# A sparse-attention and MLP kernel on one core: the whole list of steps in another order

## The chip, the cores and the metric

The kernel runs on one core of one Trainium2 chip. The metric is the device time of one execution, in microseconds (us). Five engines work beside each other, each through its own queue of instructions in order: PE (matrix products), DVE (vector work), ACT (activation functions and copies), POOL (vector work, and the issue of some DMAs), SP (the issue of the other DMAs). Sixteen DMA engines carry the transfers of both issuing queues.

## The reference: what is computed

Four batches of 8 heads, 768 positions, head size 64. Attention is local (a window of 16 positions to each side) plus 24 block keys per head (the maximum over a block of 32 keys) with block values (the mean over 32 values). Its output is 3072 tokens of width 512, which go through a two-layer MLP with a gelu in between:

```python
k_sum = k.reshape(B, H, nb, block, D).max(axis=3)
v_sum = v.reshape(B, H, nb, block, D).mean(axis=3)
scores_l = scale * q @ k^T,  kept where |i - j| < 16
scores_s = scale * q @ k_sum^T + log(32)
a = softmax(concat(scores_l, scores_s))
x = (a @ concat(v, v_sum)).transpose(0, 2, 1, 3).reshape(3072, 512)
h = x @ w_in                              # 512 -> 2048
out = (h / (1 + exp(-1.702 * h))) @ w_out # 2048 -> 512
```

## The kernel before, in words

The work goes batch by batch: turn keys and queries so that the head size lies on the partitions, scores, exponentials, values, x turned, then `x @ w_in`, gelu, and `@ w_out`. The attention of one batch is placed beside the MLP of the batch ahead of it, so that PE always has matmuls to do.

**The order is a list.** A string `ORDER` (lines 35 to 111) holds 1002 steps. The last lines of the kernel split it at blanks and call, for each word, a small function from the table `ops` with the numbers of the word as arguments. The class `_Ordered` (lines 18 to 30) wraps each engine and keeps every instruction in program order, so within an engine the list is the order of execution. Between engines only data and buffers decide. Every recorded row carries line 28, the line of the wrapper; the rows are told apart by tile names.

**The steps that the change and the prediction touch.** The first number after a name is mostly the batch.

- Loads, all issued by POOL on one software queue: `Lk`, `Lq`, `Lv` (keys, queries, values of batch 0; `load_k0`, `load_q0`, `load_v0`), `Li.0` to `Li.4` and `Lo.0` to `Lo.3` (parts of w_in and w_out), `lk.b.h`, `lq.b.h` (one head of keys or queries, 96 KB each on chip), `lv.b.j.e` (a part of the values, 64 KB). Key and query tiles of two halves are used again batch after batch. In the trace an issue on this queue waits until the one eight places ahead of it has landed.
- `gate.1`: a small POOL copy that reads the last sum row of batch 1, so that POOL issues no load behind it before that row has landed. `gate.2` does the same with the last turned x.
- `tk`, `tq` (`turn_k`, `turn_q`): keys and queries of batch 1 turned on PE; `kc`, `qc` copy them out. `xm`, `kh`, `kr`: block maxima, halos and block rows of the keys of batch 1. For batches 2 and 3 SP turns them by DMA: `xk.s.g.e` (keys, tile `kx`), `xq.s.g` (queries, tile `qT`), both for the heads of group g. There `xa.g` takes the block maxima on DVE, `ka` copies the halos, `kR` (`rows_all`) writes the maxima in.
- `s.b.half.p` (`scores`), `e` (exponentials on ACT), `m` (mask on DVE), `v.b.half.p` (values on PE, tile `ps_av`), `nn` (normed on DVE), `t`/`c` (x turned on PE and copied) or `d` (x turned by a DMA on SP).
- `vm.b` (`vsum`, 48 short matmuls) and `vb` (`block_sums`, five DVE instructions) make the block values `vs`. SP then copies them into the value tile: `sd.b.e` (sum rows) and `ha.b.i` (halo copies within the value tile `vw`). For batch 1 the list has the four halos ahead of the two sum rows. The values of a batch need all six copies.
- `f.half.nt` (`ff`): a column block of `x @ w_in`, four matmuls; `g`: its gelu on ACT.
- The product with w_out is done by seven half-size products instead of eight: `p.t.what` (`product`, 8 matmuls; tiles `poA`, `poB`, `poC`), `x.t.what` (`taken`), with sums of gelu outputs `gs.j.n.what` (`g_sums`, DVE or POOL) and of weights `ws.what.part` (`w_sum`, DVE). Product 1 and 2 need no sum; 6, 5, 7 and 3 read the sums 1, 0, 2 and 3 of all blocks, the last of which is `gs.7.1.*`. Product 2 reads the last two parts of w_out (`Lo.2`, `Lo.3`), and `ws` reads all four.
- `o`: a store on SP. `G`, `X`: the activation tables on ACT.

Of the kernel before, what the change touches and what calls it, by code (L numbers as in the profile page):

```python
# [35 lines left out]
start Lk.0 X Lk.1 id Lq.0.0 Lk.2 Lk.3 Lq.0.1 Lv.0 Lv.1 Lv.2 cs I.20.256 sel on T.0.2 Li.1 Lv.3 To.0.a ba I.2.128 km.0  # L36
sm.0.42 Li.0 sm.1.52 T.1.1 To.1.a Lq.1.0 Lq.1.1 I.3.128 Q.0.0.0 I.14.128 Qc.0.0.a Qc.0.1.d so.0 sx.0 km.1 T.2.1 To.2.a so.1
sx.1 T.3.0 em.2 ed.0 ex.0.1 ex.0.0 bt.0.1 bx.0 To.3.d Q.0.1.0 Qc.0.2.d sm.2.42 so.2 sx.2 Qc.0.3.d sm.3.52 Li.4 so.3
sx.3 km.2 vt.0.2.1 vc.0.2.d km.3 ao.0.40 ao.1.41 ab.0 ab.1 ae.1 ae.0 vn.0 vn.1 ed.1 ex.1.0 bt.1.0 ex.1.1 lh.3.g bx.1
vt.2.1.1 vc.2.1.d ao.2.2 xt.0.3 lh.0.d ab.2 xc.0.d lh.1.g ae.2 vn.2 vt.3.1.1 vc.3.1.a ao.3.1 ck.0 xt.1.3 lo.0.g lh.2.g  # L40
# [5 lines left out]
lk.1.2 lv.1.5.1 lk.1.5 lk.1.6 lq.1.2 lk.1.7 m.1.1 lq.1.1 lv.1.0.0 lq.1.4 lq.1.5 lq.1.7 lv.1.3.1 lq.1.6 lv.1.0.1
lv.1.2.0 lv.1.1.0 cv.1 lv.1.1.1 lv.1.4.0 lv.1.2.1 f.0.8.k0123.2 lv.1.4.1 late m.1.3 ws.0.0 g.0.8 f.0.9.k0123.3
f.0.11.k0123.0 g.0.9 f.0.10.k0123.1 v.0.1.0.40 v.0.1.1.41 lv.1.3.0 nn.1.0 g.0.11 lv.1.5.0 g.0.10 v.0.1.2.50 v.0.1.3.51
nn.1.1 f.0.12.k0123.2 g.0.12 f.0.13.k0123.3 g.0.13 t.1.0.42 c.1.0.d f.0.14.k0123.1 g.0.14 f.0.15.k0123.0 t.1.1.52
c.1.1.d f.1.0.k01.2 f.1.8.k01.3 f.1.1.k0123.1 ws.1.0 g.0.15 g.1.1 f.1.0.k23 ws.2.0 f.1.8.k23 g.1.0 g.1.8 ws.0.1 ws.1.1  # L50
# [30 lines left out]
x.1.3.a o.1.1.0.0.2 nn.0.1 d.0.1 p.2.1.2 x.2.1.d p.1.4 v.2.1.0.40 v.2.1.1.41 nn.1.0 x.1.4.d v.2.1.2.50 v.2.1.3.51
nn.1.1 p.2.5.1 x.2.5.a d.1.0 p.2.6 d.1.1 gate.2 lq.3.6 p.2.2.3 x.2.6.a p.2.7 x.2.7.a p.2.3 G x.2.2.a x.2.3.a
o.1.2.0.0.2 p.2.4 x.2.4.a f.0.1.k01.0 f.0.9.k01.3 f.0.0.k01.2 f.0.0.k23 xk.1.1.0 xk.1.0.1 f.0.8.k01.1 f.0.8.k23
f.0.1.k23 lv.3.5.1 lq.3.1 lq.3.2 g.0.0 g.0.8 g.0.1 o.1.1.1.0.2 f.0.9.k23 g.0.9 xk.1.1.1 xk.1.0.0 o.1.2.1.0.2 xq.1.1
f.1.0.k0123.2 g.1.0 f.1.8.k0123.1 g.1.8 f.1.1.k0123.0 xq.1.0 g.1.1 gs.0.2.2 f.1.9.k0123.3 g.1.9 f.0.2.k0123.2 g.0.2
# [879 lines left out]
```

## Time and profile before

| | |
|---|---|
| runs | 212.68, 215.77, 213.2 us; median 213.2 |
| span of the profiled execution | 212.3 us (0.4 below the lowest run) |
| PE busy | 199.1 us, 94% of the span |
| DVE, ACT, POOL busy | 127.8, 117.7, 108.6 us |
| DMA | 27.74 MB, 131 GB/s in the mean |

The page of the profile lists the busy time of each engine, then the span in 40 slices with the granted clock of PE (`PEclk`, in tenths of full speed), the DMA queues, the chain of waits (the work that ended last, followed back from the last instruction to what released it), and the costliest groups of instructions: mean duration, then the idle time of the engine ahead of them and what ended most of it. "issue" in the chain is time in which the engine waited for nothing that the profile shows. A timeline row gives the start, the length, the engine, the operation and the tiles; in brackets stands how long the engine sat idle before it and what released it. DMA rows give the time from the issue to the landing.

### The profile page before, as it was taken

How to read it: one execution, taken by the hardware profiler on the slowest of the kernel's cores; microseconds unless marked ns; L12 is line 12 of the kernel's file. 1: busy time of each engine (PE TensorE's matmuls, PEld its weight loads, DVE VectorE, ACT ScalarE, POOL GpSimd, SP SyncE). 2: the span in 40 equal slices, each digit the busy share in tenths (PEclk: the TensorE clock that was granted, in tenths of full speed). 3: DMA queues.
4: the chain of work that ended last, by engine and by line, in shares of the span. 5: the costliest groups of instructions: out<-in, count | busy, mean ns of one | idle time of the engine just before them, and what ended most of it. 6: DMA issues, size and time to landing. Idle time of an engine off the chain costs nothing.

```text
span 212.3 us, 5885 instructions
## 1 busy us (share of the span) xinstructions
PE 199.1 (94%) x2440; PEld 145.3 (68%) x2440; DVE 127.8 (60%) x311; ACT 117.7 (55%) x227; POOL 108.6 (51%) x157
## 2 busy tenths in 40 slices
PE   7888798989998899999699999999999999999992
PEld 5546555657886786656578876566888856668882
DVE  5557865799886861168976823496587602454242
ACT  2662886667865338766664048668660467670200
POOL 7999962399970989808949314331000009432000
PEclk9999999999999999999999999999999999999999
DMA  5999999999999799999999999992023930000222
GB/s 69 156 166 190 209 218 216 178 135 123 98 138 203 111 160 179 120 164 170 145 153 201 134 220 128 253 171 59 3 99 60 181 112 0 0 3 0 99 102 99
DMA packets 96458, 27.74 MB, mean 131 GB/s; under 512 B 85024, under 2 KB 93488, under 8 KB 96432
## 3 DMA queue, kind: packets, MB, share of 16 engines
q0 software_dynamic: 70800, 13.64, 85.7%
q1 hardware_dynamic: 25632, 13.74, 31.9%
q8 instruction: 19, 0.31, 0.7%
q14 instruction: 7, 0.06, 0.1%
...
## 4 chain that ended last, share of the span: by engine, by line
PE 72%; DMA 18%; POOL 4%; issue 2%; DVE 1%; SPq 0%; POOLq 0%
PE ph L28 31%; PE poA L28 19%; PE poB L28 9%; DMA w_out_sb<-in_moe_w_out_dram 7%; PE poC L28 5%; DMA kb<-in_k_dram 4%; DMA v0n<-in_v_dram 4%; DMA vw<-vs 3%; PE ps_av L28 3%; PE ps_s L28 2%; PE ps_t L28 1%; POOL kb L28 1%; PE ps_vs L28 1%; DVE vs L28 1%; POOL mk L28 1%
## 5 line engine op out<-in xcount | busy, mean ns | idle before, releaser
L28 PE MATMUL ph<-xT,w_in_sb 128*128 128x384 f16 x512 | 85.9, 326 | 0.0
L28 ACT ACTIVATE gT<-ph 128x384 f16<-128x384 f32 x128 | 58.7, 495 | 22.9 <-PE ph L28 21.9
L28 PEld LDWEIGHTS <-w_in_sb 128*128 128x128 f16 x512 | 49.2, 98 | 31.5 <-DMA w_in_sb<-in_moe_w_in_dram 0.2
L28 PEld LDWEIGHTS <-gs 128*128 128x128 f16 x384 | 36.3, 98 | 4.7
L28 DVE TENSOR_TENSOR gs<-gT 128x768 f16<-128x768 f16 (+1 forms) x36 | 17.1, 490 | 21.5 <-ACT gT L28 21.4
L28 PEld LDWEIGHTS <-gT 128*128 128x128 f16 x288 | 27.5, 98 | 3.7
L28 ACT ACTIVATE a_sb<-ps_s 128x768 bf16<-128x768 f32 x32 | 24.5, 808 | 9.1 <-PE ps_s L28 9.0
...
L28 POOL DMA_DIRECT2D kb<-in_k_dram x28 | 23.0, 836 | 8.1 <-DMA w_out_sb<-in_moe_w_out_dram 6.2
...
L28 PE MATMUL poA<-ws,gs 128*128 128x256 f16 x192 | 24.9, 273 | 0.0
L28 POOL TENSOR_TENSOR gs<-gT 128x768 f16<-128x768 f16 x4 | 6.9, 1728 | 35.0 <-ACT gT L28 35.0
L28 ACT ACTIVATE s<-poA 128x256 f32<-128x256 f32 x14 | 5.4, 384 | 20.6 <-PE poA L28 19.0
L28 DVE TENSOR_TENSOR x<-ps_av,rc 128x768 f16<-128x768 f32 (+1 forms) x18 | 15.6, 869 | 0.6
L28 DVE TENSOR_TENSOR a_sb<-a_sb,mk 128x768 bf16<-128x768 bf16 x28 | 14.6, 549 | 1.8 <-ACT a_sb L28 1.1
L28 POOL TENSOR_TENSOR gs<-gs,gT 128x768 f16<-128x768 f16 (+1 forms) x6 | 8.4, 1406 | 12.9 <-DVE gs L28 12.9
L28 DVE TENSOR_TENSOR gs<-gT,gs 128x768 f16<-128x768 f16 (+1 forms) x19 | 9.2, 490 | 7.2 <-POOL gs L28 6.6
L28 PE MATMUL poB<-ws,gs 128*128 128x256 f16 x96 | 12.5, 273 | 0.0
L28 PE MATMUL poB<-w_out_sb,gs 128*128 128x256 f16 x96 | 12.5, 273 | 0.0
L28 PE MATMUL poA<-ws,gT 128*128 128x256 f16 x96 | 12.5, 273 | 0.0
L28 PE MATMUL poC<-w_out_sb,gT 128*128 128x256 f16 x96 | 12.5, 273 | 0.0
L28 PE MATMUL poA<-w_out_sb,gT 128*128 128x256 f16 x96 | 12.3, 273 | 0.0
(102 smaller groups left out, 215.9 us busy)
## 6 DMA issues: line engine op xcount, KB each, us to landing
...
kb<-in_k_dram POOLq DMA_DIRECT2D x24, 96.0 KB, 5.7
qb<-in_q_dram POOLq DMA_DIRECT2D x24, 96.0 KB, 5.4
...
```

Of the source, the lines that this page charges most:

```text
L28: r = f(*a, **kw)
```

## The change

Only the string `ORDER` changes; it holds the same 1002 steps in another order. No function, tile, size or engine of a step is changed.

- Batch 0: all four `Lv` and both `Lq.1` are ahead of any `Li` (before: `Li.1` between `Lv.2` and `Lv.3`, `Li.0` ahead of `Lq.1`). `Lq.0.0` is behind `Lk.2`. The parts of w_in go 1, 0, 2, 3, 4 (before 1, 0, 4, 2, 3).
- w_out: `Lo.0`, `Lo.2`, `Lo.1`, `Lo.3` stand spread among the head loads of batch 1, the last of them behind sixteen (before: all four ahead of `lk.1.0`).
- Batch 1: `tk.0` and `tk.1` stand among the first steps of the second half of ff (before: in its middle); the weight sums `ws` go down to just ahead of their products. SP's copies go `ha.1.3`, `ha.1.0`, `ha.1.1`, `sd.1.1`, `ha.1.2`, `sd.1.0` (before: 3, 2, 1, 0, then the sum rows).
- Batch 2: its loads behind `gate.1` are mixed differently; `lk.2.5` is the 18th (before, the last key load was the 13th), and four parts of the values come last. First loads of batch 3 (`lv.3`) follow directly. `xk` goes 0.1.0, 0.1.1, 0.0.1, 0.0.0; two stores stand ahead of `xq.0.0`, a store and a halo ahead of `xq.0.1`. `vm.2` is six ff steps sooner. On DVE `vb`, one `gs`, `xa.0.0`, `xa.1.0`, `kR.0` stand together with most `gs` behind them; the first two scores are ahead of `p.0.1.2`.
- Batch 3: both `xa` and `kR.1` sooner, `vm.3` ten ff steps later, halos behind the sum rows or among them. In the tail the products are mixed differently; the last two steps are the same.

The diff around the keys of batches 1 and 2, cut to its core:

```diff
-sd.0.0.3 ha.0.2.3 sd.0.1.3 ha.0.3.3 ha.0.0.3 lk.1.0 f.0.0.k23 ha.0.1.3 Qc.1.3.d s.0.1.2.52 f.0.1.k01.3 e.1.2
-f.0.3.k0123.0 g.0.2 g.0.0 g.0.1 g.0.4 g.0.6 g.0.3 lk.1.3 lq.1.0 g.0.7 g.0.5 lq.1.3 ck.1 m.1.0 m.1.2 ow.1 lk.1.4 lk.1.1
-tk.0.52 kc.0.a f.1.13.k0123.0 g.1.13 ws.3.1 g.1.4 f.1.5.k0123.1 g.1.5 tk.1.52 gs.4.2.2 kc.1.a f.1.14.k0123.3 tk.2.42
-e.1.0 ha.1.1.0 x.1.1.d x.0.3.a lq.2.0 lq.2.2 lv.2.0.0 lq.2.3 kh.2.1.g p.0.4 ha.1.0.0 lv.2.5.0 o.0.0.0.0.2 x.0.4.a
-s.1.1.1.52 e.1.1 m.0.1 vm.1.42 vb sd.1.1.0 kr.2.1.g kh.3.1.d sd.1.0.0 xm.3.1 kr.3.1.d p.1.5.1 gate.1 lv.2.3.0 lv.2.1.1
-lk.2.0 m.1.1 m.0.0 lk.2.2 o.0.0.1.0.2 lv.2.2.0 lv.2.2.1 lk.2.3 lv.2.5.1 lk.2.1 x.1.5.d lk.2.4 lk.2.5 lk.2.7 lk.2.6
-g.0.0 g.0.8 g.0.1 g.0.9 xk.0.0.0 xk.0.0.1 xk.0.1.0 xk.0.1.1 xq.0.0 xq.0.1 f.1.0.k0123.2 f.1.8.k0123.1 g.1.0
-g.1.7 f.0.15.k0123.0 ha.2.3.0 g.0.15 gs.6.1.1 f.0.7.k0123.1 g.0.7 kR.0.d f.1.15.k0123.3 g.1.15 gs.7.1.0 X gs.6.1.3
-p.0.1.2 s.2.0.1.52 e.0.1 s.2.0.0.42 lv.3.1.0 lk.3.0 lk.3.4 lv.3.1.1 lk.3.2 gs.7.1.1 lk.3.7 lk.3.3 ha.2.1.0 x.0.1.d
...
+Li.3 lo.1.g mk.0 sx.3 vc.3.1.a ow.0 lk.1.0 ab.2 ae.2 vn.2 mk.1 cvs Li.4 xt.1.3 mf Qc.1.0.a ao.3.1 lv.1.1.1 cv.0 ab.3
+lk.1.1 Qc.1.3.d e.1.0 Lo.0 lq.1.0 lk.1.4 ha.0.1.3 lv.1.3.1 vo.1.d Qc.1.2.a lk.1.7 sd.0.0.3 f.0.1.k01.3 xt.3.1 s.0.1.1.42
+s.0.1.2.52 lk.1.6 xc.3.a f.0.0.k23 lq.1.1 lq.1.3 e.1.1 f.0.3.k0123.0 s.0.1.3.42 lk.1.5 f.0.2.k0123.1 Lo.2 lq.1.2 Lo.1
+g.0.14 f.0.15.k0123.0 g.0.12 t.1.1.52 t.1.0.42 f.0.13.k0123.3 c.1.1.d tk.0.52 g.0.13 c.1.0.d kc.0.a f.1.1.k0123.1
+sd.1.1.0 kr.3.1.d kh.3.1.d p.1.5.1 gate.1 p.2.1.2 ha.1.2.0 s.1.0.2.52 x.1.6.a e.0.2 s.1.0.3.42 x.1.5.d sd.1.0.0 p.1.3
+lk.2.7 f.1.9.k0123.3 g.1.0 f.1.1.k0123.0 g.1.9 lk.2.5 f.1.8.k0123.1 xk.0.1.0 f.0.2.k0123.2 g.1.8 f.1.11.k0123.3 g.0.2
+f.1.2.k0123.1 f.0.3.k0123.2 xk.0.1.1 g.1.1 g.1.11 lq.2.6 lv.2.3.1 xk.0.0.1 lv.2.2.1 f.0.10.k0123.0 g.1.2 f.1.10.k0123.3
+lv.2.5.1 g.0.3 g.0.10 lv.2.0.1 f.1.4.k0123.1 g.1.10 f.0.4.k0123.2 lv.3.2.0 f.1.12.k0123.3 f.0.11.k0123.0 g.1.4 xk.0.0.0
+o.0.1.1.0.2 gs.0.2.0 g.0.4 g.0.11 o.0.2.0.0.2 f.1.3.k0123.1 g.1.3 gs.2.2.0 vm.2.42 g.1.12 f.0.12.k0123.0 f.1.5.k0123.1
+f.0.6.k0123.2 gs.0.2.1.g g.1.13 g.0.13 g.0.6 g.1.6 vb gs.2.2.1 o.0.2.1.0.2 f.0.14.k0123.0 f.1.14.k0123.3 xa.0.0 ka.0.g
+f.1.7.k0123.2 xa.1.0 g.1.14 kR.0.d gs.4.2.2.d g.1.7 f.0.7.k0123.1 f.1.15.k0123.3 gs.4.2.0 g.0.14 gs.2.2.3 f.0.15.k0123.0
+lv.3.3.0 gs.6.1.0 ha.2.0.0 gs.6.1.1 g.0.7 g.1.15 xq.0.1 s.2.0.0.42 s.2.0.1.52 p.0.1.2 gs.7.1.0 g.0.15 gs.4.2.1 p.0.2.0
```

More of the change, by code (lines that the diff above doesn't have):

```diff
@@ L35 @@
 ORDER = """
[L36 to L40, printed above, removed]
@@ L46 @@
[L46 to L50, printed above, removed]
@@ L81 @@
[L81 to L85, printed above, removed]
@@ L106 @@
[L106 to L110 removed]
+start Lk.0 Lk.1 I.20.256 I.2.128 cs ck.1 Lk.2 id sel ba T.0.2 Lq.0.0 sm.0.42 I.3.128 To.0.a T.1.1 To.1.a Lk.3 Lq.0.1 X
@@ new lines @@
+f.0.8.k0123.2 g.0.1 lv.1.2.0 lv.1.1.0 lv.1.4.0 g.0.4 late f.0.10.k0123.1 m.1.3 f.0.11.k0123.0 g.0.10 v.0.1.0.40 lv.1.3.0
+v.0.1.2.50 v.0.1.1.41 nn.1.0 lv.1.5.0 v.0.1.3.51 nn.1.1 g.0.8 f.0.9.k0123.3 g.0.11 g.0.9 f.0.12.k0123.2 f.0.14.k0123.1
+g.0.14 f.0.15.k0123.0 g.0.12 t.1.1.52 t.1.0.42 f.0.13.k0123.3 c.1.1.d tk.0.52 g.0.13 c.1.0.d kc.0.a f.1.1.k0123.1
+f.1.0.k01.2 f.1.0.k23 f.1.8.k01.3 f.1.8.k23 g.1.1 tk.1.52 f.1.10.k0123.1 xm.0.1 g.0.15 g.1.8 g.1.0 kh.0.1.d kr.0.1.d
+ws.0.0 kc.1.a ha.1.3.0 kh.1.1.d f.1.9.k0123.0 g.1.9 lv.2.0.0 f.1.3.k0123.2 f.1.2.k0123.3 f.1.13.k0123.0 g.1.10 xm.1.1
@@ new lines @@
+gs.0.2.0 g.1.2 f.1.11.k0123.1 g.1.3 gs.0.2.2 g.1.13 f.1.12.k0123.3 f.1.4.k0123.2 tk.3.52 g.1.11 g.1.4 gs.0.2.1 tk.2.42
+f.1.5.k0123.1 gs.2.2.0 g.1.12 g.1.5 gs.2.2.2 gs.2.2.1 f.1.6.k0123.2 kc.3.d gs.0.2.3 f.1.14.k0123.3 ws.1.0 f.1.15.k0123.0
+gs.4.2.0 ws.2.0 g.1.6 gs.4.2.1 f.1.7.k0123.1 kc.2.a g.1.15 tq.0.42 g.1.14 g.1.7 p.0.1.2 tq.1.52 gs.6.1.2 ha.1.0.0
+gs.4.2.3 x.0.1.a qc.0.a gs.4.2.2 gs.7.1.0 ws.0.1 gs.6.1.0 ws.1.1 gs.6.1.1 lq.2.0 p.1.1.3 X p.0.2.0 gs.7.1.1 p.0.6
+tq.2.42 p.0.5.1 x.0.6.a gs.2.2.3 lq.2.2 gs.7.1.2 ws.2.1 p.0.7 gs.6.1.3 qc.1.a lq.2.3 ws.3.0 qc.2.a kr.1.1.d x.0.5.a
@@ new lines @@
+s.2.1.3.52 sd.2.0.0 m.1.1 e.1.3 lk.3.2 p.1.5.0 m.0.0 sd.2.1.0 x.1.1.a p.1.2.2 e.1.2 m.0.3 v.2.0.2.50 v.2.0.0.40
+v.2.0.3.51 x.1.5.d m.1.2 m.1.3 v.2.0.1.41 m.1.0 o.1.0.1.0.2 p.1.6 x.1.6.a nn.0.1 lk.3.3 x.1.2.a nn.0.0 p.1.3 p.1.7
+o.1.0.0.0.2 p.2.1.2 v.2.1.2.50 x.1.7.a G x.1.3.a v.2.1.3.51 v.2.1.0.40 v.2.1.1.41 x.2.1.d p.1.4 x.2.5.a d.0.0 p.2.6
+x.2.6.a nn.1.1 p.2.3 lv.3.1.0 lq.3.3 p.2.7 x.1.4.d lq.3.4 nn.1.0 p.2.2.3 o.1.1.0.0.2 lk.3.7 x.2.7.a d.0.1 p.2.4
+f.0.1.k01.0 x.2.2.a d.1.1 x.2.4.a f.0.9.k01.3 f.0.0.k01.2 f.0.0.k23 d.1.0 x.2.3.a g.0.0 f.0.1.k23 f.0.8.k01.1 f.0.9.k23
@@ new lines @@
+f.0.8.k23 f.1.0.k0123.2 g.0.1 lv.3.1.1 lq.3.7 g.0.8 g.1.0 f.1.1.k0123.0 lv.3.5.0 g.0.9 f.1.8.k0123.1 g.1.1 f.1.9.k0123.3
+g.1.8 f.0.10.k0123.0 f.1.2.k0123.1 xk.1.0.1 xk.1.0.0 g.0.10 f.0.2.k0123.2 lk.3.6 lv.3.0.1 o.1.2.0.0.2 xa.0.1 o.1.2.1.0.2
+g.1.9 f.1.10.k0123.3 g.1.2 lv.3.4.0 g.0.2 lv.3.3.1 g.1.10 f.1.3.k0123.1 f.0.3.k0123.2 lq.3.5 g.1.3 g.0.3 f.0.11.k0123.0
+g.0.11 f.1.11.k0123.3 f.0.5.k0123.2 f.0.12.k0123.1 g.1.11 f.1.12.k0123.3 g.0.12 g.0.5 f.1.4.k0123.0 xk.1.1.0
+f.1.5.k0123.1 g.1.12 gs.2.2.0 xk.1.1.1 xa.1.1 f.0.4.k0123.2 g.1.4 f.1.14.k0123.3 g.1.5 gate.2 g.0.4 g.1.14 f.1.6.k0123.1
@@ new lines @@
+f.0.6.k0123.2 g.0.6 lv.3.5.1 f.0.13.k0123.0 f.1.13.k0123.3 g.0.13 kR.1.d f.0.7.k0123.2 g.1.13 lq.3.2 f.0.14.k0123.0
+lq.3.1 ha.3.0.0 g.0.7 vm.3.52 g.0.14 ka.1.d f.1.15.k0123.3 g.1.6 gs.0.2.0.d gs.0.2.1 f.0.15.k0123.0 f.1.7.k0123.1
+o.1.1.1.0.2 gs.4.2.0 p.0.1.2 g.1.7 g.1.15 gs.0.2.2 lq.3.6 gs.4.2.1 g.0.15 X xq.1.0 s.3.0.1.42 gs.2.2.1.g vb gs.6.1.0
+gs.4.2.3 gs.6.1.1 gs.7.1.2 gs.7.1.0 xq.1.1 x.0.1.d s.3.0.0.52 sd.3.1.0 sd.3.0.0 p.0.5.1 gs.4.2.2 gs.0.2.3 gs.7.1.1.g
+p.0.2.3 x.0.2.a x.0.5.d p.0.6 gs.7.1.3 gs.2.2.3 gs.6.1.2 gs.2.2.2.g p.1.1.3 ha.3.3.0 e.0.0 e.0.1 gs.6.1.3 m.0.1 x.1.1.d
@@ new lines @@
+f.1.14.k0123.3 f.0.13.k0123.0 g.1.14 f.0.6.k0123.2 f.1.6.k0123.1 g.0.13 g.0.6 gs.4.2.0.g g.1.6 f.0.14.k0123.0
+f.0.7.k0123.2 g.0.14 gs.6.1.2.d f.1.7.k0123.1 gs.4.2.2.d gs.6.1.0.d f.0.15.k0123.0 f.1.15.k0123.3 gs.6.1.1 g.1.7 g.0.7
+gs.4.2.1 g.1.15 gs.6.1.3 g.0.15 gs.7.1.0 gs.4.2.3 p.0.1.2 p.0.5.1 gs.7.1.2 gs.0.2.2.g gs.7.1.1.g x.0.1.d p.0.2.0 p.0.6
+p.1.1.3 x.0.2.a gs.0.2.3.d p.2.2.0 gs.2.2.3 gs.7.1.3.g x.0.6.a p.0.7 x.0.5.d p.0.3 x.0.7.a x.0.3.a o.3.0.0.0.2 p.0.4
+x.1.1.a p.1.6 x.0.4.a p.1.5.1 p.1.2.2 x.1.5.d x.1.6.a o.3.0.1.0.2 x.1.2.a p.1.7 p.2.1.2 p.1.3 x.2.1.d x.1.3.a p.2.6
@@ L111 @@
+x.1.7.a p.2.5.1 x.2.6.d x.2.5.a p.2.7 x.2.7.a o.3.1.0.0.2 p.2.3 p.1.4 x.2.2.a x.2.3.a x.1.4.d o.3.2.1.1.2 p.2.4
+o.3.2.0.0.2 x.2.4.d P7.0 o.3.1.1.0.2 o.3.2.1.0.1
 """
```

80 lines of the change are left out of this document (29 added, 51 removed).

## The prediction, as put on record before the result

> **What bounds the kernel now.** I read the page's first two sections first, then busy time by stretches, the chain of waits, and last the queue of SP and the rows of DVE, POOL and DMA around the three places at which the chain leaves PE.
>
> ```profile
> span 212.3 us, 5885 instructions
> PE 199.1 (94%) x2440; PEld 145.3 (68%) x2440; DVE 127.8 (60%) x311; ACT 117.7 (55%) x227; POOL 108.6 (51%) x157
> PEclk9999999999999999999999999999999999999999
> ```
>
> PE is busy 199.1 of 212.3 us at full granted clock. The change neither adds nor removes an instruction, so only PE's idle 13.2 us can shrink, and a new order pays only where PE waits.
>
> ```profile
> 0.00:31.00 31.00, 26.02 (x437) 17.45 (x438) 21.16 (x76) 17.90 (x33) 27.78 (x57) 1.00 1.36 166
> ```
>
> 5.0 of the 13.2 lie in the first 31 us (second number: PE busy), in a dozen waits of at most 1.3 us; nearly 4 lie behind the last matmul, where the change only swaps products. The rest stands in the chain of waits:
>
> ```profile
> 21.24 15.14 DMA w_out_sb<-in_moe_w_out_dram
> ...
> 36.66 9.09 DMA kb<-in_k_dram
> 45.75 0.05 issue
> 45.80 0.51 PE ps_t L28 x6
> ...
> 63.86 5.72 DMA vw<-vs
> 69.58 0.04 issue
> 69.63 0.64 PE ps_av L28 x24
> ...
> 95.67 0.53 PE ps_vs L28 x48
> ...
> 101.73 1.78 issue
> 103.52 0.70 PE ps_s L28 x24
> ...
> 108.38 0.87 PE poB L28 x8
> ...
> 169.45 20.80 PE ph L28 x128
> ```
>
> Columns: start, length, what. Three places matter: the turn of batch 1's keys (`tk.0`, 45.80), the first values of batch 1 (`v.1.0.0`, 69.63) and the first scores of batch 2 (`s.2.0.1`, 103.52, after 1.78 us of idle). How long PE stood at the first two is told by these two rows, from the table of tile kb and from the list of waits:
>
> ```profile
>   PE ps_t L28: 0.6, 1
> ```
>
> ```profile
> PE ps_av L28 <- DMA vw<-vs: 1.3, 1, 1.3
> ```
>
> So 0.6, 1.3 and 1.8 us are to be had there. From 104 us to the end PE waits for almost nothing. The last chain row prices a step: 128 matmuls of ff in 20.80 us, 0.65 for each step `f` of four; a product is 0.87.
>
> **The change part by part.** All times are against the profiled execution's 212.3 us. It lies 0.4 below the lowest run (212.68) and 0.9 below the median (213.2); I add 0.9 at the end.
>
> 1. *Head: values ahead of w_in, other order of the first loads.* Every load of batch 0 and w_in goes through POOL's one queue, and none is dropped. `Lq.0.0` goes behind `Lk.2`, so the first queries land later by one load; the values land sooner and w_in's parts later. I walked PE's steps to `f.0.12` by the landings of the trace: PE gets there 0.3 us later than before. The bounds are -1 (the values' part of the 5.0 us goes) and +1.5 (w_in is late for ff). I take +0.3, since the two moves offset each other.
>
> 2. *Keys of batch 1.* The first chain rows show why `tk.0` waited: `lk.1.1` was issued only at 36.66, when the queue's w_out part had landed 15.14 us after its issue. After the change four of batch 1's keys go ahead of any `Lo`, so `lk.1.1` should land near 38; `tk.0` moves ten ff steps earlier (6.5 us), to about 39. Its 0.6 goes. Late next is w_out.
>
> ```profile
> GB/s 69 156 166 190 209 218 216 178 135 123 98 138 203 111 160 179 120 164 170 145 153 201 134 220 128 253 171 59 3 99 60 181 112 0 0 3 0 99 102 99
> ```
>
> The last part (`Lo.3`) now stands behind 16 head loads of batch 1. When `lk.1.1` landed before (45.75), all of w_in and w_out and 6 head loads were down, so `Lo.3` lands about 10 head loads behind that: 96 KB each at the 218 to 135 GB/s of the slices there (5.3 us each) are 0.44 to 0.7 us, which makes 50 to 53. Its first users are `ws.1.1` and `p.0.2.0`, near 53.2 (`tk.0` at 39, then 14.2 us of PE's steps in the new order): margin 0 to 3 us, cost 0, and one for one if it is later than that. Moving `ws` down costs nothing on PE as long as DVE is not late; the one place where it is, by my walk, is `gs.7.1.3` ahead of `p.0.3`: +0.3.
>
> 3. *Sum rows ahead of halos, batch 1.* `vb` ends a little earlier, `sd.1.1` is issued ahead of `ha.1.2`, `sd.1.0` behind it. Issue to landing took 5.72, so `sd.1.0` lands near 69.7, as before: it is the last of the eight that `v.1.0.0` needs. But one product more (0.87) is done ahead of `v.1.0.0`, so of the 1.3 us wait about 0.5 is left. PE stands 0.8 better after it; the waits of steps 1 and 2 disappear into this one.
>
> 4. *Loads of batch 2 and the key turns on SP.* All loads of batch 2 come behind `gate.1`. In the new order the last key load (`lk.2.5`) is the 18th behind the gate; it was the 13th.
>
> ```profile
> 69.48 1.36 POOL L28 DMA_DIRECT2D vw<-in_v_dram  x2
> ```
>
> ```profile
> L28 POOL DMA_DIRECT2D kb<-in_k_dram x28 | 23.0, 836 | 8.1 <-DMA w_out_sb<-in_moe_w_out_dram 6.2
> ```
>
> ```profile
> kb<-in_k_dram POOLq DMA_DIRECT2D x1, 96.0 KB, 5.0
> ```
>
> (The last row is one key load issued at 78.7.) The gate opens 0.5 sooner, near 69.0. 6 value loads by 0.68 and 12 others by 0.84 make 14.2 us: the 18th is issued by 83.2, or 84 with one wait for a free place on the queue, and lands near 88.5. Only then does SP start the four `xk`.
>
> ```profile
> 80.53 9.58 SPq L28 DMA_TRANSPOSE kx<-kb  x4
> ...
> 126.07 3.52 SPq L28 DMA_TRANSPOSE kx<-kb  x2
> ...
> 130.60 3.19 SPq L28 DMA_TRANSPOSE kx<-kb  x2
> ```
>
> ```profile
> DMA to landing us min/median/max: 3.9/6.4/9.6
> ```
>
> (Tile kx.) In batch 3 the fourth `xk` was issued 5.9 us behind the first (126.07 to about 132.0). With a landing of 3.9 to 9.6 the four take 9.8 to 15.5 us. I take 10, near the low end, because that is the 9.8 of batch 3, and because most loads of batch 2 are now down ahead of the transposes. Keys turned: 98.5.
>
> ```profile
> 91.66 1.75 DVE L28 TENSOR_REDUCE ka<-kx 128x48 bf16<-128x1536 bf16 x1 [0.60 <-DMA kx<-kb]
> ...
> 96.11 1.75 DVE L28 TENSOR_REDUCE ka<-kx 128x48 bf16<-128x1536 bf16 x1 [1.76 <-DMA kx<-kb]
> ...
> 103.11 0.52 DVE L28 COPY kx<-ka 128x576 bf16<-128x576 bf16 x2
> ```
>
> Two maxima and the rows, 1.75 + 1.75 + 0.5 = 4.0, now stand directly behind one another, where before there were 5.2 us of `gs` and `vb` between the second maximum and `kR`. Keys ready: 102.5. The scores now go ahead of `p.0.1.2` (0.87), so the same pace as before means a start at 103.52 - 0.87 = 102.65. PE's own arrival: `vm.2` has six ff steps (3.9) less ahead of it and the 0.8 of step 3, so PE reaches it at 95.67 - 3.9 - 0.8 = 91.0, when the last value load (the 23rd) lands between 91 and 93; from there 9.1 us of work lead to the scores: 100 to 102. Queries: `xq.0.0` goes behind the four `xk` and two stores, issued near 97, lands near 102; `xq.0.1`, behind a store and a halo copy more, near 105, for `s.2.0.2` at 106.7. Keys and queries come within a microsecond of each other, PE is there a little sooner. I take the scores at 102.9, +0.25: the 1.8 us wait does not vanish, it is taken up by the later keys, and so is the gain of step 3.
>
> 5. *What DVE has put off.* The `gs` that stood ahead of `kR` now stand behind it.
>
> ```profile
> L28 DVE TENSOR_TENSOR gs<-gT 128x768 f16<-128x768 f16 (+1 forms) x36 | 17.1, 490 | 21.5 <-ACT gT L28 21.4
> ```
>
> From `kR.0` to `gs.7.1.3`, which `p.0.3` reads, there are 15 `gs` (7 of two parts at 0.49, 8 of one part at some 0.28) and two `x` of 0.41: 6.5 us. From 102.9 that gives 109.4, against 108.38 when `p.0.3` started before: +1.0 in place of the 0.25. Bounds: 0 (keys 1 us sooner) and +3 (keys 2 us later).
>
> 6. *Rest of batches 2 and 3, tail.* The `d` transposes of batch 2 have their two `nn` swapped and a store between: the last xT needed lands about when PE asks for it, 0 to +1, I take +0.4. In batch 3 `vm.3` goes 6.5 us of work later with `vb` behind it, and the three first products stand closer to their `gs`: 0 to +0.5, +0.2. The tail keeps its last product, store and wait: 0.
>
> Sum behind the scores of batch 2, which swallow all that was gained ahead of them: +1.0 + 0.4 + 0.2 = +1.6. Span 213.9; run 214.8, rounded down to 214.5 because two of the three terms have zero as their lower end.
>
> **Rivals.**
>
> *A. Slower: keys of batch 2 too late.* Mechanism: 18 loads ahead instead of 13, and the four transposes on SP beside the last value loads and the first of batch 3, which are now issued early. If the four take 13 us (half way between 9.8 and 15.5), keys are ready at 88.5 + 13 + 4.0 = 105.5, `gs.7.1.3` at 112.0, `p.0.3` 3.6 late; with step 6, +4.2: 217.4, and 219.5 at 15.5. For it speaks the 9.6 us landing beside loads in batch 2, against it 3.9 in batch 3. It decides from a fourth landing at about 101.
>
> *B. The same with a slower clock.* In A PE stands some 3.5 to 4.5 us ahead of the scores. If PE came back from such a gap at half clock for as long as the gap was, it would lose half of that again, about 2 us: 219.5. No row here shows it: the longest gap in the chain is 1.78 us and PEclk is 9 in all 40 slices. The Trainium skill, "TensorE: Matmul & The Clock Gate", section "HAM oscillation — how this bites in real kernels", warns of PE gaps over about 3.4 us, after which the clock is halved; it speaks against this change where A holds, and the trace can't confirm it, since no gap of that length lies between its matmuls.
>
> *C. Faster.* All three waits go (0.6 + 1.3 + 1.8) and the load order holds: keys turned by 96, `xq` in time, `gs` in time. 213.2 - 3.7 = 209.5; with 1 us of the head, 208.5. For it: the long chain pieces of DMA are exactly what the order attacks. Against it: the keys' last load is later, not sooner.
>
> *D. w_out late.* `Lo.3` lands at 55 to 56: PE waits 2 to 3 at `p.0.2.0`. But `v.1.0.0` waits 0.5 anyway; the sum rows follow PE's `vm.1`, so they slip as well, and the loads of batch 2 behind them: +2 to +3 on all of it, 217.
>
> *E. Nothing nets:* each wait is replaced by one as long, 213.2.
>
> **How the numbers follow.** Forecast (212.3 to 216.5) 0.48; A 0.18; B 0.05; C 0.12; D 0.07; E, within the forecast's own band, 0.10. The prediction is 214.5. Two per cent, 208.9 and 217.5, is about what a measurement of this kernel can tell from no change. Faster by over 2%: less than the whole of C, since 209.5 itself is within it: 0.08. Slower: B, most of A, a third of D, and a tail of the forecast: 0.27. The remaining 0.65 is within 2%. The range leaves out the far ends of A and B and of C: 210.0 to 219.0.
>
> **What would show it.** Right: `tk.0` waits for nothing; `v.1.0.0` waits about half a microsecond for a sum row; the last key load of batch 2 lands at 88 to 89; the first maximum of batch 2 starts at 98 to 99 and both stand back to back; the scores of batch 2 start near 103 and `p.0.3` behind them waits about 1 us for DVE. Wrong: the fourth `xk` lands behind 101 (A); PE's granted clock drops behind a gap (B); no idle over 0.5 us at any of the three places (C); `p.0.2.0` of batch 0 waits for `w_out_sb` (D).

## The result, and the profile after

The changed kernel takes 221.39 us (median of 219.36, 221.09, 221.69 and 223.06) against 213.19 before: a ratio of 1.033, 95% interval 1.024 to 1.042. The forecast was 214.5, with a range of 210.0 to 219.0. The ratios, and the times of the experiments below (medians), leave out executions in a slower state, to which the profiled one (223.06 us, span 221.4) belongs, so a second profile of the same kernel (span 219.9, `changed_again` below) stands beside it.

The page of the changed kernel:

```profile
span 221.4 us, 5878 instructions
PE 203.3 (92%) x2440; PEld 147.6 (67%) x2440; DVE 128.0 (58%) x311; ACT 115.8 (52%) x227; POOL 109.1 (49%) x157
PEclk9999999999799999999969999999999999999999
```

Two things differ from before. PE's idle time is 18.1 us and not 13.2. And PE is busy 4.2 us longer with the same 2440 matmuls: in two slices the granted clock is below full. So 9.1 us divide into 4.9 of waiting and 4.2 of longer work. In the second profile PE is busy 203.4 us and idle 16.5: its 7.6 us are 3.3 of waiting and 4.2 of longer work.

Waits of PE, changed kernel (total, times, longest):

```profile
PE ps_s L28 <- DMA qT<-qb: 5.8, 2, 4.4
PE poA L28 <- DMA w_out_sb<-in_moe_w_out_dram: 2.2, 1, 2.2
```

These are the two new waits: the scores of batch 2 for the turned queries, and the first product of batch 0 for w_out. The three waits of before are gone or small: `tk.0` runs at 39.3 without a wait, `v.1.0.0` waits for nothing, `kR.0` is in time. PE's timeline at the two places, two rows each:

```profile
51.42 0.60 PE L28 MATMUL poA<-w_out_sb,gT 128*128 128x256 f16 x4
54.27 0.60 PE L28 MATMUL poA<-w_out_sb,gT 128*128 128x256 f16 x4 [2.25 <-DMA w_out_sb<-in_moe_w_out_dram]
...
112.99 0.82 PE L28 MATMUL ps_s<-qT,kx 64*128 64x64 bf16 x24 [4.41 <-DMA qT<-qb]
113.74 1.89 PE L28 MATMUL poA<-ws,gs 128*128 128x256 f16 x8
```

The product of 8 matmuls takes 1.89 us in the last row, where such a row takes 1.04 or 1.05 at full clock. The busy times by stretches, whose third number from the end is the granted clock, show why:

```profile
55.00:58.00 3.00, 3.00 (x18) 2.25 (x16) 1.35 (x4) 2.52 (x4) 1.14 (x3) 0.50 2.17 161
58.00:58.50 0.50, 0.50 (x6) 0.40 (x4) 0.50 (x3) 0.00 (x0) 0.41 (x1) 0.82 2.40 152
...
113.00:116.00 3.00, 3.00 (x35) 2.30 (x36) 0.56 (x1) 1.79 (x3) 1.83 (x3) 0.50 1.65 140
116.00:116.50 0.50, 0.50 (x6) 0.38 (x5) 0.00 (x0) 0.10 (x1) 0.50 (x1) 0.79 1.43 226
```

Finer windows put the two stretches of half clock at 54.77 to 58.18 and at 112.80 to 116.21, 3.41 us each. PE does half its work in such a stretch, so each costs about 1.7 us and the two together some 3.3, most of the 4.2.

The table shows PE's lost time at some steps: the start of the step in the trace, less the median durations of all PE steps ahead of it in that kernel's order. It counts waits and the slow clock alike. The numbers in the heads are the spans.

| us lost up to | before (212.3) | changed (221.4) | changed again (219.9) |
|---|---|---|---|
| `f.0.12`, end of the head | 6.2 | 6.9 | 7.9 |
| `p.0.1.2` of batch 0 | 7.0 | 7.0 | 7.9 |
| `vm.1` | 7.4 | 11.3 | 9.2 |
| `vm.2` | 9.8 | 11.9 | 10.7 |
| `s.2.0.0` | 11.8 | 13.5 | 10.8 |
| `v.2.0.0` | 12.0 | 19.6 | 18.3 |
| the last product | 12.5 | 21.7 | 20.3 |

The loss has two steps, from `p.0.1.2` to `vm.1` (4.3 us in one profile, 1.3 in the other, 0.4 before) and from `s.2.0.0` to `v.2.0.0` (6.1 and 7.5; 0.2 before). What was gained between, from `vm.1` to `vm.2` (2.4 us lost before, 0.6 and 1.5 after), is 1.8 and 0.9 us, far less than the two steps.

SP's and POOL's queues about the second place, changed kernel:

```profile
98.34 1.58 SPq L28 DMA_TRANSPOSE qT<-qb  x1
100.01 1.06 SPq L28 DMA_DIRECT2D out_dram<-osb  x1
101.17 0.61 SPq L28 DMA_DIRECT2D vw<-vw  x1
101.95 4.47 SPq L28 DMA_TRANSPOSE qT<-qb  x1
```

```profile
100.92 1.68 POOL L28 DMA_DIRECT2D kb<-in_k_dram  x2
104.75 0.82 POOL L28 DMA_DIRECT2D qb<-in_q_dram  x1 [2.14 <-DMA qT<-qb]
105.56 1.66 POOL L28 DMA_DIRECT2D kb<-in_k_dram  x2
```

```profile
qT<-qb SPq DMA_TRANSPOSE x1, 10.9
```

The second transpose of the queries was issued at 101.95 and landed 10.9 us later, and its issue alone took 4.47 where the first took 1.58. Beside it POOL issues loads of batch 3. In the kernel before the landings of the query transposes took these times, for batches 2 and 3 together:

```profile
DMA to landing us min/median/max: 4.4/4.8/7.2
```

The keys came as forecast: the last key load landed near 90, the four `xk` took 8.3 us, and DVE shows both maxima back to back and the rows behind them:

```profile
99.05 3.41 DVE L28 TENSOR_REDUCE ka<-kx 128x48 bf16<-128x1536 bf16 x2 [1.56 <-DMA kx<-kb]
102.49 0.53 DVE L28 COPY kx<-ka 128x576 bf16<-128x576 bf16 x2
```

### The profile page after: what moved, and what is told of

Its sections match the earlier page's. It is cut to its first block, busy times and chain, and to the rows that moved or that the text cites. A ratio compares the mean times of both kernels' runs of the same rounds, so it can differ in the third digit from the quotient of the medians.

```text
span 221.4 us, 5878 instructions
## 1 busy us (share of the span) xinstructions
PE 203.3 (92%) x2440; PEld 147.6 (67%) x2440; DVE 128.0 (58%) x311; ACT 115.8 (52%) x227; POOL 109.1 (49%) x157
## 5 line engine op out<-in xcount | busy, mean ns | idle before, releaser
L28 ACT ACTIVATE gT<-ph 128x384 f16<-128x384 f32 x128 | 57.4, 493 | 28.2 <-PE ph L28 27.5
L28 PEld LDWEIGHTS <-gs 128*128 128x128 f16 x384 | 37.1, 99 | 5.7 <-issue 0.3
L28 ACT ACTIVATE a_sb<-ps_s 128x768 bf16<-128x768 f32 x32 | 24.6, 809 | 18.3 <-PE ps_s L28 18.1
L28 PEld LDWEIGHTS <-gT 128*128 128x128 f16 x288 | 28.2, 101 | 7.8 <-issue 3.5
L28 PE MATMUL poA<-ws,gs 128*128 128x256 f16 x192 | 25.8, 279 | 0.1
L28 POOL DMA_DIRECT2D kb<-in_k_dram x28 | 23.6, 867 | 3.3 <-DMA w_out_sb<-in_moe_w_out_dram 2.2
L28 PE MATMUL poA<-w_out_sb,gT 128*128 128x256 f16 x96 | 13.5, 285 | 3.2 <-DMA w_out_sb<-in_moe_w_out_dram 2.2
L28 ACT ACTIVATE s<-poA 128x256 f32<-128x256 f32 x14 | 5.4, 383 | 18.3 <-PE poA L28 17.6
L28 PE MATMUL ps_s<-qT,kx 64*128 64x64 bf16 x336 | 8.3, 195 | 7.0 <-DMA qT<-qb 5.8
L28 PEld LDWEIGHTS <-kx 64*128 64x128 bf16 x336 | 6.3, 97 | 10.4 <-issue 9.9
L28 PE MATMUL poC<-w_out_sb,gT 128*128 128x256 f16 x96 | 13.1, 281 | 0.0
L28 DVE TENSOR_REDUCE ka<-kx 128x48 bf16<-128x1536 bf16 x4 | 6.9, 1748 | 9.7 <-DMA kx<-kb 9.7
```

Source lines behind the costliest of these rows:

```text
L28: r = f(*a, **kw)
```

## The experiments

The theory after the result: both steps of the loss are waits for a DMA, each followed by a stretch of half clock; nothing else in the new order costs much. Three questions divide this theory from its rivals. Is the w_out wait a matter of where `Lo` stands (P) or of a queue that runs half empty (Q)? Do the queries come late by their place on SP's queue (S) or by the loads beside them (L)? And does the clock fall because PE stood still (C)?

**Undoing the w_out wait, two ways.** Both are the changed order with the loads of batch 1 put differently. The diff is cut: only loads and mask steps are shown, and the steps between them are left out.

```diff
 w_out_sooner
-lk.1.0 lv.1.1.1 lv.1.0.0 lk.1.3 lv.1.4.1 lk.1.2 lk.1.1 Lo.0 lq.1.0 lk.1.4 lv.1.3.1 lk.1.7 lk.1.6 lq.1.1 lq.1.3 lk.1.5 Lo.2 lq.1.2 Lo.1 Lo.3
+lk.1.0 lk.1.3 lk.1.2 lk.1.1 Lo.0 lk.1.4 lk.1.7 lk.1.6 lk.1.5 Lo.1 lq.1.0 lq.1.1 Lo.2 Lo.3 lq.1.2 lq.1.3 lv.1.1.1 lv.1.0.0 lv.1.4.1 lv.1.3.1
 queue_full
+mk.0 lk.1.0 lk.1.3 lk.1.2 lk.1.1 Li.4
+mk.1 Lo.0 Lo.1
+mf lk.1.4 lk.1.7 lk.1.6 lk.1.5 Lo.2 Lo.3
+Q.1.1.0 lq.1.0 lq.1.1 lq.1.3 lq.1.2 lv.1.1.1 lv.1.0.0 lv.1.4.1 lv.1.3.1 ...
```

In queue_full all other loads of batch 1 follow directly behind these, in their old sequence.

> The changed order, with w_out's last three parts pulled ahead of most query and value loads of batch 1 (Lo.0, four keys, Lo.1, two queries, Lo.2, Lo.3). Theory of place (P): PE stood 2.25 us in p.0.1.2 for Lo.1, and its clock was halved behind that; both go, nothing else was late, so 4 us less than the changed kernel (about 217 us). Rival (Q, the queue): the head loads of batch 1 end 4 us later than before (last value load 64.5 against 60.3) because POOL puts small loads one by one into a queue that runs half empty from 25 to 43 us; moving Lo alone only shifts who is last: p.0.1.2 waits for nothing, but vm.1 then waits 2 to 4 us for the values, and the gain is 0 to 2 us (219 to 221).

> The changed order, with four keys and Li.4 ahead of POOL's second mask step, Lo.0 and Lo.1 ahead of its last, the other keys and Lo.2, Lo.3 right behind it, then queries and values: large transfers are in the queue while POOL computes the masks. P: as with w_out sooner, 4 us less than the changed kernel. Q: the last value load of batch 1 lands near 60 again and not near 64, vm.1 waits for nothing, 4 us less, and 2 to 4 us better than w_out sooner. If both versions gain the same 4 us, Q falls.

Measured: w_out_sooner 216.95 us, ratio to before 1.021 (1.010 to 1.032); queue_full 216.65, ratio 1.016 (1.003 to 1.028). In w_out_sooner the product waits for nothing, but PE's timeline shows who is late next:

```profile
62.23 0.31 PE L28 MATMUL ps_vs<-vw,E 64*32 64x128 bf16 x16 [1.11 <-DMA vw<-in_v_dram]
64.15 0.25 PE L28 MATMUL ps_vs<-vw,E 64*32 64x128 bf16 x8 [1.61 <-DMA vw<-in_v_dram]
```

`vm.1` waits 2.7 us in all for the values, as Q said. In queue_full it waits for nothing:

```profile
61.47 0.60 PE L28 MATMUL ps_vs<-vw,E 64*32 64x128 bf16 x48
```

The rate of the transfers from 26 to 43 us (last number, GB/s) fits this. The three lines are before, changed and queue_full; w_out_sooner had 171.

```profile
26.00:43.00 17.00, 16.24 (x160) 10.04 (x158) 11.29 (x29) 12.16 (x26) 7.75 (x16) 1.00 1.46 204
```

```profile
26.00:43.00 17.00, 15.98 (x175) 10.32 (x175) 8.65 (x22) 13.33 (x28) 14.47 (x26) 1.00 1.52 152
```

```profile
26.00:43.00 17.00, 15.15 (x169) 9.78 (x169) 8.07 (x21) 12.26 (x26) 14.55 (x29) 1.00 1.57 189
```

Before, four parts of w_out of 512 KB each were in the queue while POOL built the masks; in the changed order POOL puts in loads of 64 and 96 KB, 0.7 to 0.85 us apiece. Over these 17 us, 52 GB/s less are some 0.9 MB, almost two parts of w_out. That the small loads are the cause of the lower rate is read from these rows; no run changed their size alone.

So P is right about the wait, and Q about what the wait was worth: moving `Lo` alone trades it for one at `vm.1`. The time that P gave, about 217, came out, but not for its reason: in w_out_sooner's profile the queries' wait is 2.0 us with the clock full, and from `s.2.0.0` to `v.2.0.0` it loses 2.1 us where the changed kernel lost 6.1 and 7.5. Nothing in the edit aims at that place. Q's last point, that queue_full be 2 to 4 us better, is not shown: the intervals overlap. queue_full's mask came late for `v.0.1.0` (1.2 us), and it waits 3.8 us for queries.

**Undoing the queries' wait, two ways.** The diff shows the steps that move; those between them are left out.

```diff
 queries_sooner
-xk.0.0.0 o.0.1.1.0.2 o.0.2.0.0.2 xq.0.0 o.0.2.1.0.2 ha.2.0.0 xq.0.1
+xk.0.0.0 xq.0.0 xq.0.1 o.0.1.1.0.2 o.0.2.0.0.2 o.0.2.1.0.2 ha.2.0.0
 loads_later
-lv.3.3.0 lk.3.0 lk.3.1 lq.3.0 lk.3.4 lk.3.5 lv.3.4.1 lk.3.2 lk.3.3 lv.3.1.0 lq.3.3 lq.3.4
+lq.3.0 lq.3.4 lv.3.3.0 lk.3.0 lk.3.1 lk.3.4 lk.3.5 lv.3.4.1 lk.3.2 lk.3.3 lv.3.1.0 lq.3.3
```

> The changed order, with xq.0.0 and xq.0.1 directly behind the four xk on SP's queue, ahead of three stores and a halo. Theory S (SP's order): xq.0.1 was issued at 102 and landed at 113 because it stood behind stores and next to the first loads of batch 3; issued near 98.5 it lands by 104, the waits ahead of s.2.0.0 (1.4) and s.2.0.2 (4.4) go, PE keeps its full clock there (1.9): 6 to 7.5 us less than the changed kernel, about 214. Rival L (loads of batch 3 are the cause, wherever xq.0.1 stands): it lands 10 us behind its issue again, near 108.5, and 2 us of the wait stay: 3 to 4 us less, about 217.5.

> The changed order, but lq.3.0 and lq.3.4 stand ahead of the other loads of batch 3; both wait for the query tiles that xq reads, so POOL issues no load beside xq.0.1. SP's order is as changed (stores and a halo ahead of xq.0.1). S (SP's order alone): xq.0.1 still is issued at 102 and s.2.0.2 still waits 4 us: no gain. L (loads beside it): xq.0.1 is down 5 to 6 us behind its issue and not 10.9, near 108, the wait of 4.4 falls to under 1 and the half clock behind it goes: 4 to 6 us less than the changed kernel; loads of batch 3 then come 8 us later, which may cost up to 1 us.

Measured: queries_sooner 217.08, ratio 1.018 (1.011 to 1.025); loads_later 217.60, ratio 1.020 (1.014 to 1.026). In both profiles neither score waits for queries. SP's rows and the landing in loads_later:

```profile
99.60 1.07 SPq L28 DMA_DIRECT2D out_dram<-osb  x1
100.77 0.61 SPq L28 DMA_DIRECT2D vw<-vw  x1
101.54 1.74 SPq L28 DMA_TRANSPOSE qT<-qb  x1
```

```profile
qT<-qb SPq DMA_TRANSPOSE x1, 4.3
```

The issue stands at the same place of SP's queue as in the changed kernel, 0.4 us sooner, and takes 1.74 and not 4.47; the landing comes after 4.3 and not 10.9. So the place alone is not enough for the wait, against S: with batch 3's loads away the stores ahead do no harm. The loads alone are not enough either, against L: queries_sooner leaves them where they were, issues at 99.2 and lands after 5.9. The wait needs both, a late place and the loads beside it; taking away either is enough.

Each gains some 4 us. For queries_sooner 6 to 7.5 had been expected. It fits that the w_out wait in its profile is 3.2 us, longer than in the changed kernel's own, with a stretch of half clock behind it (54.65 to 58.06). In loads_later that wait is 2.9 us without a fall of the clock, and PE waits 1.4 us more for x of batch 2, which a DMA turns.

**The clock by itself.** Useless matmuls keep PE busy where it waited; their results are overwritten. Every wait for DMA stays. The diff is cut to the added lines and the heads of their functions.

```diff
+F.18 p.0.1.2
+F.25 s.2.0.2.42
 def product(t, what, where=None):
+    for _ in range(st.pop("fill", 0)):
+        pe.matmul(out=po, lhsT=w_in_sb[:, 0, 0:128], rhs=w_in_sb[:, 0, 0:N1], start=True, stop=True, skip_group_check=True)
 def scores(b, half, p, where):
+    for _ in range(st.pop("fill", 0)):
+        pe.matmul(out=big[:, 0:HALF], lhsT=w_in_sb[:, 0, 0:128], rhs=w_in_sb[:, 0, 0:HALF], start=True, stop=True)
```

> The changed order, with useless matmuls on w_in (18 of 256 columns ahead of p.0.1.2, 25 of 384 columns ahead of s.2.0.2) that only keep PE busy where it waited for DMA; results are overwritten. Theory C (the granted clock falls because PE stood): PEclk stays 1.00 behind both places, the products there take 0.87 again and not 1.4 to 1.9, and 3.5 us go although every wait for DMA stays: about 217.5. Rival (the clock falls for another reason, such as the load on the chip at that place): the clock is 0.50 there again, no gain, 221.

Measured: 219.49 (219.24 to 219.75), ratio 1.029 (1.022 to 1.036); profile 217.9:

```profile
PEclk9999999999999999999999999999999999999999
```

```profile
107.06 4.23 PE L28 MATMUL ps_s<-w_in_sb 128*128 128x384 f16 x25
111.22 0.52 PE L28 MATMUL ps_s<-qT,kx 64*128 64x64 bf16 x24
111.67 1.05 PE L28 MATMUL poA<-ws,gs 128*128 128x256 f16 x8
```

The scores still come at 111.2, but the product behind them takes 1.05 and not 1.89, and the clock is full everywhere. So at these two places C holds as a mechanism: with PE filled the clock does not fall, though the DMA waits are there. What this is worth is less sure. The runs differ by 1.6 and 2.0 us (219.49 against 221.09 and 221.49), with intervals that overlap, so the gain is not clear of the noise; the profiled spans differ by 3.5, but 221.4 is the longest of its four runs.

**The changed kernel again.**

> The changed kernel, unchanged, beside the others of this set: 219.5 to 221.5 by the runs so far. Its profile should show the same two places, p.0.1.2 waiting 2 to 3 us for w_out and the scores of batch 2 waiting 4 to 6 us for queries, with PEclk 0.50 behind any wait of more than 2 us.

Measured: 221.49 (219.61 to 221.97), ratio 1.039 (1.033 to 1.045). PE at the second place, and the clock there:

```profile
110.54 0.82 PE L28 MATMUL ps_s<-qT,kx 64*128 64x64 bf16 x24 [4.58 <-DMA qT<-qb]
111.30 1.89 PE L28 MATMUL poA<-ws,gs 128*128 128x256 f16 x8
112.98 1.91 PE L28 MATMUL poB<-w_out_sb,gs 128*128 128x256 f16 x8
```

```profile
110.00:116.40 6.40, 5.86 (x68) 4.12 (x69) 0.98 (x2) 2.93 (x5) 3.85 (x5) 0.50 2.13 148
```

The queries' wait is as long, and the half clock behind it lasts twice as long. The w_out wait was only 0.5 us here, without a fall of the clock: PE came 0.9 us later (the head had lost more) and `Lo.1` landed 0.8 sooner. Of the two expectations the one for the queries (4 to 6 us) was met, the one for w_out (2 to 3) was not. The second place is thus the steady part of the loss; the first varies from 0.5 to 3.2 us over the profiles of kernels with the same loads of batch 1.

**Both undone.** queue_full and queries_sooner in one order:

> queue_full and queries_sooner together. If the two places are all of the loss, the gains add: 221.1 - 2.7 - 4.0 = 214.4 by the medians, or less, since queue_full alone still waited 3.8 us for queries in its profile: 212 to 214.5, about as before. If the queries' place only hides another limit (sum rows of batch 2, stores), v.2.0 waits 1 us or more and the time stays above 215.

Measured: 214.08, ratio 1.005 (1.002 to 1.009). In its profile (211.3) the two places are free:

```profile
100.39 0.52 PE L28 MATMUL ps_s<-qT,kx 64*128 64x64 bf16 x24
100.85 1.05 PE L28 MATMUL poA<-w_out_sb,gT 128*128 128x256 f16 x8
101.73 1.04 PE L28 MATMUL poC<-w_out_sb,gT 128*128 128x256 f16 x8
102.61 1.91 PE L28 MATMUL poB<-ws,gs 128*128 128x256 f16 x16
104.45 0.52 PE L28 MATMUL ps_s<-qT,kx 64*128 64x64 bf16 x24
```

So the two places hold nearly all of the loss: 7 of 8 us. What is left of the change is still 0.5% slower than before, although its keys now come without any wait. The longest wait in this profile stands in the head, where the values of batch 0 wait for a halo copy; up to `f.0.12` this profile loses 2.2 us more than the one before:

```profile
PE ps_av L28 <- DMA vw<-vw: 1.8, 1, 1.8
```

**Two attempts to go below that.** best is both with two mask steps sooner (`mk.1` ahead of `lk.1.1` and `Li.4`, and the last one, `mf`, ahead of `Lo.0`), the three stores of batch 1 ahead of the `xk`, and in batch 3 two of DVE's sums behind `x.0.2`. both_and_takes is both with the last of these alone:

```diff
-p.0.5.1 gs.4.2.2 gs.0.2.3 gs.7.1.1.g p.0.2.3 x.0.2.a x.0.5.d
+p.0.5.1 gs.7.1.1.g p.0.2.3 x.0.2.a x.0.5.d gs.4.2.2 gs.0.2.3
```

> As both, with three more moves: the last mask step ahead of Lo.0 (in queue_full v.0.1.0 waited 1.2 us for a mask), the three stores of batch 1 ahead of the xk instead of behind the xq (sum rows of batch 2 come 2 us sooner), and two of DVE's sums in batch 3 behind x.0.2 (p.1.1.3 waited 0.9 us). 1.5 to 2.5 us less than both: 210.5 to 212, one per cent better than before. If it is no better than both, those waits had cover that now is gone.

> both, with the two DVE sums in batch 3 behind x.0.2 and x.0.5: p.1.1.3 waited 0.95 us for x.0.2 in every profile of the changed order. 0.5 to 1.0 us less than both: equal to before within 0.3%. If the sums are then late for p.0.7 or p.0.3, no gain.

Measured: best 215.65, ratio 1.014 (1.009 to 1.019), which does not beat both and looks worse; both_and_takes 213.82, ratio 1.004 (1.000 to 1.008), not told from both. In best the transfers of w_out are issued late again, and the stretch from 26 to 43 us has 162 GB/s where both has 189:

```profile
33.16 1.51 POOL L28 DMA_DIRECT2D w_out_sb<-in_moe_w_out_dram  x2
```

```profile
26.00:43.00 17.00, 14.94 (x175) 9.37 (x175) 8.57 (x22) 11.59 (x24) 13.77 (x27) 1.00 1.29 162
```

They went out at 30.0 in both. My reading is that the long mask work was cover for the queue, not a delay to it: with loads issued ahead of it the queue stayed full meanwhile. Which of best's moves costs the time was not run apart, and its profile also has a fall of the clock early in the head. The wait of `p.1.1.3` (0.95) is gone from both profiles without a gain in the runs that can be told.

**One part of the change alone, in the order before.** rows_sooner moves one step, rows_and_products three, six_steps seven. Dots stand for steps left out.

```diff
 rows_sooner
-xa.1.0 gs.2.2.0 ... gs.6.1.1 f.0.7.k0123.1 g.0.7 kR.0.d
+xa.1.0 kR.0.d gs.2.2.0 ... gs.6.1.1 f.0.7.k0123.1 g.0.7
 rows_and_products, further
-v.1.0.0.50 m.1.3 v.1.0.1.51 p.1.4 x.1.4.a o.0.1.1.0.2 p.2.5.1 x.2.5.a
+p.1.4 p.2.5.1 v.1.0.0.50 m.1.3 v.1.0.1.51 x.1.4.a o.0.1.1.0.2 x.2.5.a
 six_steps, further
-lk.1.4 lk.1.1
+lk.1.1 lk.1.4
-vm.2.42 g.1.13 g.0.6 gs.4.2.0 gs.4.2.2.d vb
+vm.2.42 vb g.1.13 g.0.6 gs.4.2.0 gs.4.2.2.d
-gs.6.1.0 ... gs.6.1.1 ... gs.7.1.0 X gs.6.1.3 ... gs.7.1.1 ... x.0.1.d
+gs.6.1.0 ... gs.7.1.0 gs.6.1.1 X ... gs.7.1.1 ... x.0.1.d gs.6.1.3
```

> The order before the change, with one part of the change alone: kR.0 directly behind xa.1.0 on DVE, ahead of the sums and vb (one step moved, 0.52 us). In before, the scores of batch 2 waited 1.78 us for it. If that wait was the only thing in the way, the queries are down (100.97) and the sums are in time (gs.7.1.3 ended 1.6 us ahead of p.0.3), 1.3 to 1.8 us go: ratio 0.992 to 0.994. Rival: the next wait (queries, or p.0.3 for its sum) takes over, 0 to 0.5 us.

> As rows_sooner, and p.1.4 and p.2.5.1 ahead of v.1.0.0 (the change did one product more there), so that 1.74 us of PE's work cover the 1.32 us wait for the last sum row. Another 0.8 to 1.3 us: ratio 0.987 to 0.990. Rival: normed values of batch 1 come later against PE's turns of x, which wait instead: no gain over rows_sooner.

> The order before the change, with rows_and_products and four more single steps: lk.1.1 ahead of lk.1.4 (tk.0 waited 0.6 for it), vb of batch 2 directly behind vm.2 (in rows_and_products a score waited 0.4 for its bank), gs.6.1.1 behind gs.7.1.0 and gs.6.1.3 behind x.0.1 (p.0.5 waited 0.3 and p.0.6 0.7 us for DVE). If these waits were the last ones at their places, another 0.8 to 1.5 us: ratio 0.986 to 0.991, clear of no change. Rival: each is replaced by the next wait behind it, as with rows_sooner, and the ratio stays at 0.993 to 0.997.

Measured: rows_sooner 212.40, ratio 0.997 (0.993 to 1.001); rows_and_products 211.73, ratio 0.995 (0.991 to 1.000); six_steps 211.71, ratio 0.996 (0.992 to 1.000). All three stand within half a per cent of the order before. six_steps is 0.4% faster than it, at the edge of what can be measured. The rival of each expectation held: the wait that was removed is gone, and others have come. PE's waits in six_steps:

```profile
PE poB L28 <- DVE osb L28: 0.8, 1, 0.8
PE poA L28 <- DVE s L28: 0.7, 1, 0.7
PE poB L28 <- DVE gs L28: 0.7, 1, 0.7
```

2.2 us, for DVE each time, stand where 3.7 for keys, sum rows and DVE had stood.

## Why the prediction was wrong, point by point

The direction was right, and so was it that later waits swallow the gains ahead of them. The steps that failed are step 4's queries ("near 105", which is some 5 us from issue to landing, where the landings took 10.2 and 10.9) and step 2's "cost 0" for w_out (PE waited 0.5 to 3.2 us, at a reader that the walk did not have). The half clock behind these two waits was in no term of the sum at all.

1. Head: forecast +0.3, bounds to +1.5; measured +0.7 and +1.7 in the two profiles, and +0.4 to +0.5 in those of queries_sooner, loads_later and pe_filled, which have the same head. So the forecast was near. In the +1.7 stands a wait of 1.2 us of the first values for a halo copy (0.6 before, 0.3 in the first profile), which the walk did not have.
2. Keys of batch 1: right, `tk.0` waits for nothing. The w_out part of this step failed: "lands near" 50 to 53, "first users ws.1.1 and p.0.2.0", "cost 0". There were two errors. The first user of a late part is `p.0.1.2`, 2 us sooner: product 1 reads the first half of w_out, and `Lo.1` stands next to last in the new order. The prediction followed only `Lo.3`. And the loads came later than their sum said: `Lo.1` landed at 54.2 and 53.4, `Lo.3` itself at 55.7 and 56.8. From 26 to 43 us they moved 152 GB/s and not 204, with 0.7 to 0.85 us of POOL for each issue of a head load. Rival D (0.07) had w_out late and 217, but for `Lo.3` at `p.0.2.0`.
3. Sum rows: right. `v.1.0.0` waits 0 and 0.3 us (forecast 0.5). The copies that it needs are six, not eight; nothing hangs on that.
4. Keys of batch 2: right in each part: last load 88.9 and 90.5 (88.5), four `xk` 8.2 and 8.3 us (10), rows written by 101.2 and 103.0 (102.5). The queries failed. The text has `xq.0.1` "near 105, for s.2.0.2 at 106.7", which is 5 us from issue to landing. It landed at 112.9 and 110.4: 10.9 and 10.2. The prediction shows no row for the queries' landing. The trace before had 4.4 to 7.2 us, and one issue that took 4.91, so the dear case could be seen there. For the keys the dear row, 9.6 beside loads, was quoted in the same step, and rival A used it. But the new order moves the contention: keys turn when the loads are down, queries turn when batch 3's loads have begun, for these too stand sooner. The page that the Trainium skill calls "DMA: Bandwidth & Descriptors", section "Issuing engines are not separate DMA queues", says that DMAs from SP and POOL share the same engines and interleave; the runs agree (4.3 us with batch 3's loads away, 10.9 beside them).
5. DVE's sums: `gs.7.1.3` ended at 109.8 and 108.0 (forecast 109.4). Right, and worth nothing, for PE stood until 110.5 to 113 for the queries.
6. Rest: the last xT was no wait (forecast +0.4); batch 3 cost 1.1 and not 0.2, the tail 0.3 and not 0. `p.1.1.3` waits 0.95 for DVE, where a sum took 1.99 us (from 157.11) instead of 0.55, while POOL ran a sum of its own of 1.95 us from 156.73.

Two numbers of the working were off besides. It added 0.9 us from the profiled span to the time of a run. In every later execution, of the kernel before too, the time is 1.65 to 1.78 above its own span (223.06 against 221.4; 212.40 against 210.7 before), so this term was some 0.8 too small. And rival A at 15.5 us for the four `xk` gives 219.9 by its own sum, not 219.5.

The term that was not in the sum at all is the clock. Rival B asked for a gap of 3.5 us or more and had a chance of 0.05. Behind gaps of 2.25, 2.33 (queue_full), 3.16 (queries_sooner) and 4.4 to 4.6 the clock was halved. The two falls of 3.41 us in one profile of the changed kernel cost about 1.7 us each, the one of 6.8 in the other about 2.9, for there PE came back only 1 us after it began. The gap need not be as long as the Trainium skill, "TensorE: Matmul & The Clock Gate", section "HAM oscillation — how this bites in real kernels", says (about 3.4 us). That the stretch of half clock is 3.4 us, or twice that, agrees with the window of 3413 ns that the page gives in Part 1. The measurement decides on the first: with 2.94 us in loads_later the clock stayed full, with 2.25 in the changed kernel it fell, so length alone doesn't tell it.

The traces show what tells these two apart. In each of them the changes of the clock stand whole multiples of 3.41 us apart (full stretches of 47.79, 54.61 and 102.40 us, which are 14, 16 and 30 of them). Counted off from such a change, the window just ahead of the fall in the changed kernel has PE busy for 1.16 of 3.41 us, a third. The gap of 2.94 us in loads_later is cut in two by a window's end, and both windows have PE busy for half or more:

```profile
51.36:54.77 3.41, 1.16 (x14) 0.90 (x12) 2.86 (x7) 0.53 (x2) 0.85 (x2) 1.00 1.24 204
```

```profile
50.42:53.83 3.41, 1.73 (x16) 1.20 (x15) 2.39 (x5) 1.49 (x4) 1.53 (x2) 1.00 1.14 175
53.83:57.25 3.42, 2.15 (x22) 1.90 (x22) 2.21 (x6) 1.45 (x3) 0.69 (x1) 1.00 1.63 187
```

The other windows ahead of a fall behind a long gap have PE busy for 0.00 (the second place, both profiles), 0.19 (queries_sooner) and 0.39 (queue_full) of their length. So it mattered where in the window the gap lay. This is read from the traces; no run moved a gap within a window, and one early fall in best, behind a window of 0.53, does not fit a fixed limit.
